# Gate and up products: two half-height terms placed in row tiles of the TensorE array

## The chip, the cores and the metric

The kernel runs on one core of one Trainium2 chip. The metric is the device time of one launch in microseconds (us). A core has TensorE (PE in the profile; its weight loads have a row of their own, PEld), VectorE (DVE), ScalarE (ACT), GpSimd (POOL) and SyncE (SP), which issues most of the transfers. TensorE multiplies a stationary operand of up to 128 rows by 128 columns (the weights, loaded by an instruction of their own) with a moving operand, whose columns stream through, and adds into PSUM.

## The reference

The whole computation is float32, S = 2048 tokens, D = 448, a hidden width of 1792:

```
a, b = xn @ dft_hid_re.T, xn @ dft_hid_im.T          # xn = layernorm(x)
h    = x + dft_seq_re @ a - dft_seq_im @ b
hn   = layernorm(h)
out  = h + (gelu(hn @ w_gate) * (hn @ w_up)) @ w_down   # gelu: tanh form
```

The change lies in the two products `hn @ w_gate` and `hn @ w_up`, which contract over 448.

## The kernel before, in words

**Numbers.** Every float32 operand is split into a float16 high part and a float16 low part (`hi_part` on ACT, `lo_part` on DVE). A product is the sum of high times high, high times low and low times high, each a float16 matmul into the same PSUM accumulator.

**Stages.** First the two Fourier products (lines L626, L498 and L691), until about 346.7 us of the span. Then gate and up (L1014), with the down product (L962) woven in from the second quarter on. Then a tail in which the last down products run alone (L1177, L1219).

**Gate and up.** The tokens are taken in four quarters (`q`) of 512, the hidden width in 14 slices of 128 for gate and for up (`f`). One pair of these is a unit `t`, 56 in all. A unit is a 2 by 2 block product: gate and up by two halves of the contraction, times those halves by two groups of 256 tokens. It is done in seven products of blocks (a Strassen form), added up in three PSUM accumulators X, Y and Z of 128 by 256. The class `GateUp` holds a unit; `product` (from L1002) writes the matmuls of one block product.

**Two kinds of product.** The contraction of 448 is cut into 256 and 192. A product over 256 has six matmuls: two slots of 128 rows times three terms. A product over 192 has one slot of 128 rows and a rest of 64 rows. Its operand on the token side is laid out in three slots: 128 rows of high part; one slot that holds the high part of the last 64 in one half of its rows and their low part in the other; 128 rows of low part. On the weight side the last 64 rows stand twice, one below the other. So one matmul with the mixed slot does high times high and high times low of the rest at once. The five terms are in `product`:

```
terms = [(0, 0, 0), (1, 0, 0), (0, 1, 1), (1, 1, 1), (0, 0, 2)]   # weight part, weight slot, token slot
```

The term (1, 1, 1) multiplies the low weights of the last 64 rows, both copies, with the mixed slot: low times high, which is needed, and low times low, which is of the size of the rounding.

**The order around the change.** The kernel is scheduled by hand: each engine executes its instructions in the order in which the Python code issues them. From the second quarter on, the PE of a unit runs: `z_open` (Z, six matmuls), eight matmuls of the down product, `xy` (Y six, X five), ten of the down product, `yz` (Y five, Z five), three of the down product, then `open` of the next unit (X six, Y six). In the first quarter there is no down product between them, and units alternate between two sets of banks; after it there is one bank each for X, Y and Z, so the next unit's first matmul on Y waits until the last reading of Y is done. `yz` runs the products A22 by T4 into Y and S4 by B22 into Z, then DVE adds Y to a kept sum (`plus(c21, ...)`, L1024), POOL multiplies it by the activated gate (L1081), and in `c12_plus` DVE reads Z (L1024 again).

**The token operands.** `ffn_hi` and `ffn_lo` fill a tile `xs` with the high and low parts, eight times in all (four quarters by two groups); `ffn_transpose` turns it by a DMA into `hops`, where rows are the contraction. T4 is the third of the three 192-row operands.

Of the kernel before, what the change touches and what calls it, by code (L numbers as in the profile page):

```python
# [32 lines left out]
def kernel(  # L33
# [40 lines left out]
    V, A, G, PE = nc.vector, nc.scalar, nc.gpsimd, nc.tensor  # L74
# [31 lines left out]
    def hi_part(dst, src, scale=1.0):  # L106
        A.activation(dst, src, AF.Copy, scale=scale)  # L107

    def lo_part(dst, src, hi, scale=1.0):
        if isinstance(scale, float) and scale == 1.0:  # L110
            V.tensor_sub(dst, src, hi)  # L111
        else:
            V.scalar_tensor_tensor(dst, src, scale, hi, op0=ALU.mult, op1=ALU.subtract)  # L113
# [43 lines left out]

    OPS_K1 = {"B11": 0, "T1": 4, "T2": 8, "T3": 12}  # L160
    OPS_K2 = {"B21": 16, "B22": 19, "T4": 22}
    N_OPS = 25
# [90 lines left out]
    def ffn_views(q, j):  # L253
        xn, t, xs = ffn[q, j]
        k1 = xs[:, 0:2048].rearrange("p (o h d) -> p o h d", o=4, h=2)
        k2 = xs[:, 2048:3200].rearrange("p (o d) -> p o d", o=3)
        return xn, t, k1, k2, t[:, 0:768].rearrange("p (o d) -> p o d", o=3)

    def ffn_hi(q, j, parts=range(2)):
        if 0 in parts:  # L260
            ffn[q, j] += (fops.tile([P, N_OPS * P], F16, tag="xs", name=f"xs_{q}_{j}"),)
        xn, t, k1, k2, t3 = ffn_views(q, j)
        if 0 in parts:
            hi_part(k1[:, 0, 0, :], xn[:, 0, 0:256])
            hi_part(k2[:, 0:2, 0:192], xn[:, :, 256:448])
        if 1 in parts:
            hi_part(k1[:, 1:4, 0, :], t3)
            hi_part(k2[:, 2, 0:192], t[:, 768:960])

    def ffn_lo(q, j, parts=range(5)):  # L270
        xn, t, k1, k2, t3 = ffn_views(q, j)
        raw, t4 = (k2[:, 0:2], xn[:, :, 256:448]), (k2[:, 2], t[:, 768:960])
        if 0 in parts:
            lo_part(k1[:, 0, 1, :], xn[:, 0, 0:256], k1[:, 0, 0, :])
        if 1 in parts:
            lo_part(k1[:, 1:4, 1, :], t3, k1[:, 1:4, 0, :])
        for n, (dst, src) in ((2, raw), (4, t4)):
            if n in parts:
                lo_part(dst[..., 192:256], src[..., 128:192], dst[..., 128:192])
            if min(n + 1, 4) in parts:  # L280
                lo_part(dst[..., 256:384], src[..., 0:128], dst[..., 0:128])

    def ffn_split(q, j):
        ffn_hi(q, j)
        ffn_lo(q, j)
# [432 lines left out]
    for k, f in enumerate(reversed(range(NF))):  # L718
        n = (17, 20, 22, 25, 27, 30, 33, 35, 38, 40, 43, 45, 48, 50)[k]
# [8 lines left out]
    for p, (n, half) in enumerate(turns):  # L728
        b, j = divmod(p, 2)
        m = (19, 24, 29, 36, 44, 52, 60)[p]  # L730
# [59 lines left out]
    first = [(jj, part, g) for jj in range(2) for part in range(2) for g in range(2)]  # L790
    for n in range(N_STEPS):
# [41 lines left out]
        if n >= FAST:  # L833

            last = n % 4 == 3
# [163 lines left out]

    TQ = 2 * P  # L1000

    def product(ps, q, t, a, b, first, last):  # L1002

        w, ops = gw[t].rearrange("p (l o d) -> p l o d", l=2, o=14), hops[q]
        wa = W_OPS[a]
        if b in OPS_K1:
            m = OPS_K1[b]

            terms = [(0, 1, 0), (0, 0, 1), (1, 1, 0), (1, 0, 1), (0, 1, 2), (0, 0, 3)]
        else:  # L1010
            m = OPS_K2[b]
            terms = [(0, 0, 0), (1, 0, 0), (0, 1, 1), (1, 1, 1), (0, 0, 2)]
        for n, (wl, ws, ms) in enumerate(terms):
            PE.matmul(  # L1014
                ps,
                w[:, wl, wa + ws, :],
                ops[:, m + ms, :],
                start=first and n == 0,
                stop=last and n == len(terms) - 1,
                skip_group_check=True,  # L1020
            )

    def plus(dst, ps, other):
        V.scalar_tensor_tensor(dst, ps, SC, other, op0=ALU.mult, op1=ALU.add)  # L1024
# [6 lines left out]
    class GateUp:  # L1031
# [9 lines left out]
            pool, tag = (ps_gu, "XYZ"[k]) if self.own else (ps_dn, f"a{k}")  # L1041
            return pool.tile([P, 512], F32, tag=tag, name=f"p{'XYZ'[k]}_{self.name}")[:, :TQ]

        def mul(self, ps, a, b, first):
            product(ps, self.q, self.t, a, b, first, True)

        def open(self):
            self.X, self.Y = self.bank(0), self.bank(1)
# [25 lines left out]
            return hh[self.q][:, n, 2 * k + g, :]  # L1074

        def yz(self):
            self.mul(self.Y, "A22", "T4", False)
            self.mul(self.Z, "S4", "B22", False)
            c21 = self.hidden(0)
            plus(c21, self.Y, self.u1)  # L1080
            G.tensor_mul(c21, c21, self.g1)  # L1081
# [64 lines left out]
    last = {}  # L1146
# [98 lines left out]
    for q in (2, 3):  # L1245
        for j in range(2):
            t0 = (q - 1) * NF + 6 * j
            for f, k, what in (
                (0, 1, lambda q=q, j=j: ffn_norm_act(q, j, hp[q, j])),
                (1, 1, lambda q=q, j=j: ffn_sums(q, j, (0,))),  # L1250
                (1, 2, lambda q=q, j=j: ffn_sums(q, j, (1,))),
                (2, 1, lambda q=q, j=j: ffn_sums(q, j, (2,))),
                (2, 1, lambda q=q, j=j: ffn_hi(q, j, (0,))),
                (2, 2, lambda q=q, j=j: ffn_sums(q, j, (3,))),
                (2, 2, lambda q=q, j=j: ffn_lo(q, j, (0,))),
                (3, 1, lambda q=q, j=j: ffn_hi(q, j, (1,))),
                (3, 2, lambda q=q, j=j: ffn_lo(q, j, (1,))),
                (4, 1, lambda q=q, j=j: ffn_lo(q, j, (2,))),
                (4, 2, lambda q=q, j=j: ffn_lo(q, j, (3,))),
                (5, 1, lambda q=q, j=j: ffn_lo(q, j, (4,))),  # L1260
                (4, 4, lambda q=q, j=j: ffn_transpose(q, j, (0,))),
                (5, 4, lambda q=q, j=j: ffn_transpose(q, j, (1,))),
                (6, 4, lambda q=q, j=j: ffn_transpose(q, j, (2,))),
                (6, 5, lambda q=q, j=j: ffn_transpose(q, j, (3,))),
            ):
                at(side, (t0 + f, k), what)

    for t in range(3 * NF, N_GU):
        f = t % NF
        if f < NF - 1:  # L1270
            n, k = divmod(f, 2)
# [36 lines left out]
    for t in range(N_GU):  # L1308
        q, f = divmod(t, NF)
# [117 lines left out]
    for k in range(7):  # L1427
        for n in range(4, NC):
            last_pair_mm(k, n, banks)
        for m, dst, sign in users.get(k, ()):  # L1430
            bank, c = banks[m]
            h, ps = drain.x[dst], bank[:, c * HD : (c + 1) * HD]
# [64 lines left out]
```

## Time and profile before

| | |
|---|---|
| median of 3 runs (lowest to highest) | 714.15 us (713.4 to 714.18) |
| the profiled execution's own time | 713.42 us |
| its span, first to last instruction | 711.6 us, so 1.8 us lie around it |
| PE busy | 706.2 us, 5517 matmuls and as many weight loads |
| granted TensorE clock, mean | 0.999 |
| gate and up, first to last matmul of L1014 | 346.7 to 678 us |

Rows of the profile have this form: line, engine, operation, output and inputs by the program's names, tile sizes, count, then busy time, the mean of one in ns, idle time before, and what ended it. A row of a timeline has the start in us and the length in us from the first start to the last end of the instructions merged in it. The end of a matmul in the records is modelled: a matmul's record is longer than the distance to the next matmul's start, because several are in the array at once. What a matmul costs in a dense stream is the distance of starts.

### The profile page before, as it was taken

Reading aid. Unit: us, or ns where it says so; the run is one execution under the profiler, and the core shown is the slowest. Engines: PE = TensorE matmul, PEld = TensorE weight load, DVE = VectorE, ACT = ScalarE, POOL = GpSimd, SP = SyncE. Lnnn points to the kernel's source line nnn. Section 1 sums busy time; section 2 is a strip of 40 time slices with the busy share of each in tenths; the row PEclk is TensorE's granted clock in tenths of the full one; section 3 lists DMA queues with packets and bytes.
Section 4 is the critical chain, followed back from the end, with each engine's and each line's share of the span. In section 5 each row is a group of like instructions: output and inputs, shape, how many; then the busy total and the mean of one; then the engine's idle time right before and its main releaser. Section 6 shows DMA issues by size and latency. Waiting matters only on the chain.

```text
span 711.6 us, 14303 instructions
## 1 busy us (share of the span) xinstructions
PE 706.2 (99%) x5517; PEld 535.6 (75%) x5517; DVE 571.5 (80%) x1194; ACT 323.5 (45%) x612; POOL 235.5 (33%) x277
## 2 busy tenths in 40 slices
PE   9999999999999999999999999999999999999998
PEld 5555555555555555897978899999999999999998
DVE  7997638696958979999667788787787877989787
ACT  5776524263617554543335444442444434354331
POOL 0000000000000000000365866576686766858441
PEclk9999999999999999999999999999999999999999
DMA  8788558999999999653698425648448576555401
GB/s 270 251 258 257 113 181 222 299 321 259 275 334 292 303 295 226 261 136 103 163 385 306 158 79 167 189 163 203 176 136 249 183 210 212 187 215 208 156 28 53
DMA packets 102613, 150.92 MB, mean 212 GB/s; under 512 B 61072, under 2 KB 72464, under 8 KB 102544
## 3 DMA queue, kind: packets, MB, share of 16 engines
q1 hardware_dynamic: 102400, 149.09, 68.0%
q10 hardware_dynamic: 144, 0.92, 0.4%
q8 instruction: 43, 0.70, 0.4%
q14 instruction: 26, 0.21, 0.1%
HBM read 115.90 MB, written 20.19 MB: 191 GB/s over the span
## 4 chain that ended last, share of the span: by engine, by line
PE 95%; DVE 2%; issue 1%; ACT 1%; DMA 0%; ACTq 0%; DVEq 0%
PE acc L626 33%; PE pY L1014 15%; PE acc_d L962 12%; PE pZ L1014 9%; PE pX L1014 9%; PE y L691 8%; PE acc_f L498 3%; PE last_a L1219 2%; PE last_X L1177 1%; PE last_tr L1177 1%; ACT ws L107 1%; DVE e L526 0%; DMA x<-in_x_dram 0%; DVE sums L452 0%; DVE sums L453 0%
## 5 line engine op out<-in xcount | busy, mean ns | idle before, releaser
L626 PE MATMUL acc<-xs,ws 128*128 128x448 f16 x1248 | 237.9, 352 | 0.3 <-DVE affine L372 0.3
L626 PEld LDWEIGHTS <-ws 128*128 128x128 f16 x1248 | 122.0, 98 | 114.3 <-ACT ws L107 0.4
L1014 PEld LDWEIGHTS <-gw 128*128 128x128 f16 x1755 | 171.5, 98 | 17.1
L209 POOL TENSOR_TENSOR wd_s<-wd 128x448 f32<-128x448 f32 x7 | 8.0, 1142 | 351.1 <-DMA wd<-in_w_down_dram 341.6
L1014 PE MATMUL pY<-hops,gw 128*128 128x256 f16 x765 | 105.3, 273 | 0.0
L962 PE MATMUL acc_d<-wd,dn_w 128*128 128x224 f16 x882 | 105.1, 259 | 0.0
L962 PEld LDWEIGHTS <-dn_w 128*128 128x128 f16 x882 | 85.0, 98 | 2.9
L113 DVE SCALAR_TENSOR_TENSOR ws<-wr,ws 128x1024 f16<-128x1024 f32 (+2 forms) x66 | 75.1, 1139 | 7.5 <-ACT ws L107 7.2
L107 ACT ACTIVATE ws<-wr 128x1024 f16<-128x1024 f32 (+2 forms) x66 | 64.4, 980 | 31.2 <-DMA wr<-in_w_seq_dram 29.6
L1024 DVE SCALAR_TENSOR_TENSOR u<-pY,u 128x256 f32<-128x256 f32 x112 | 46.9, 419 | 30.5 <-ACT c L1088 18.9
L1014 PE MATMUL pX<-hops,gw 128*128 128x256 f16 x495 | 68.7, 273 | 0.0
L1014 PE MATMUL pZ<-hops,gw 128*128 128x256 f16 x495 | 68.4, 273 | 0.0
L691 PE MATMUL y<-wh,z 128*128 128x448 f16 x336 | 66.2, 352 | 0.7 <-DVE hx L701 0.7
L1065 ACT ACTIVATE g<-pX 128x256 f32<-128x256 f32 x56 | 21.4, 382 | 81.4 <-PE pX L1014 74.2
L1052 ACT ACTIVATE u<-pX 128x256 f32<-128x256 f32 x56 | 21.4, 383 | 80.8 <-PE pX L1014 80.7
L691 PEld LDWEIGHTS <-z 128*128 128x128 f16 x336 | 32.9, 98 | 30.5 <-issue 0.9
L111 DVE TENSOR_TENSOR dn_w<-dn_s,dn_w 128x640 f16<-128x640 f32 x42 | 52.8, 1258 | 1.1 <-ACT dn_w L107 0.8
L1081 POOL TENSOR_TENSOR hh<-hh,g 128x256 f32<-128x256 f32 x42 | 31.0, 739 | 55.7 <-DVE hh L1024 53.2
L498 PEld LDWEIGHTS <-ws 128*128 128x128 f16 x504 | 48.3, 98 | 0.9
L1090 POOL TENSOR_TENSOR hh<-hh,c 128x256 f32<-128x256 f32 x42 | 38.2, 908 | 17.9 <-ACT c L1088 17.9
L1107 POOL TENSOR_TENSOR dn_s<-hh 128x256 f32<-128x256 f32 x42 | 43.7, 1040 | 0.0
L1108 POOL TENSOR_TENSOR dn_s<-hh 128x256 f32<-128x256 f32 x42 | 43.3, 1030 | 0.0
(144 smaller groups left out, 1017.5 us busy)
## 6 DMA issues: line engine op xcount, KB each, us to landing
gw<-w_dram SPq DMA_DIRECT2D x45, 896.0 KB, 5.0
wr<-in_w_seq_dram SPq DMA_DIRECT2D x100, 256.0 KB, 4.9
w_dram<-gu_w SPq DMA_DIRECT2D x14, 896.0 KB, 6.7
gu_raw<-in_w_gu_dram SPq DMA_DIRECT2D x28, 384.0 KB, 6.0
wr<-in_w_seq_dram SPq DMA_DIRECT2D x14, 512.0 KB, 5.4
wd<-in_w_down_dram SPq DMA_DIRECT2D x14, 448.0 KB, 3.9
gw_first<-w_dram SPq DMA_DIRECT2D x7, 896.0 KB, 5.6
x<-in_x_dram SPq DMA_DIRECT2D x16, 224.0 KB, 3.1
```

The lines of the kernel that those rows point to most:

```text
L107: A.activation(dst, src, AF.Copy, scale=scale)
L111: V.tensor_sub(dst, src, hi)
L113: V.scalar_tensor_tensor(dst, src, scale, hi, op0=ALU.mult, op1=ALU.subtract)
L498: PE.matmul(fast_sum(n, k), fast_a(n, i, lw, a), fast_b(j, lx, b), start=j == 0 and m == 0 and k % 2 == 0, stop=j == NT // 2 - 1 and m == ...
L626: PE.matmul(acc[key][:, :D], w[:, lw, block * P : (block + 1) * P], xs[c][:, lx, :], start=c == 0 and m == 0, stop=c == NT - 1 and m == 2,)
L691: PE.matmul(y[:, :D], z[p][:, lz, k, g * P : (g + 1) * P], wh[:, lw, k, :], start=k == 0 and m == 0, stop=k == 6 and m == 2,)
L962: PE.matmul(acc[k // 2][:, k % 2 * HD : (k % 2 + 1) * HD], a_of(la, a), b_of(lb, b), start=first and m == 0 and k % 2 == 0, stop=last and ...
L1014: PE.matmul(ps, w[:, wl, wa + ws, :], ops[:, m + ms, :], start=first and n == 0, stop=last and n == len(terms) - 1, skip_group_check=True,)
L1024: V.scalar_tensor_tensor(dst, ps, SC, other, op0=ALU.mult, op1=ALU.add)
L1090: G.tensor_mul(c22, c22, self.c12)
L1107: G.tensor_add(s[:, 0:2], t[:, 0:2], t[:, 2:4])
L1108: G.tensor_sub(s[:, 2:4], t[:, 1:4:2], t[:, 0:4:2])
```

## The change

Of the two products in `yz`, the term (1, 1, 1) is taken out of the five. The four others of Y run, then the four others of Z, and behind them two matmuls of 64 rows instead of two of 128: one for Y in rows 64 to 127 of the array, one for Z in rows 0 to 63, each with the low weights of the last 64 rows and only the high part of the tokens. The low times low part of the last 64 rows is thus left out in these two products. The two matmuls use different rows of the array and different PSUM accumulators.

So that Y's high part lies in rows 64 to 127, T4's mixed slot is turned round: low part in its first half, high part in its second. B22 and B21 keep theirs. The high parts of T4, which were one ACT instruction of 192 columns, become two of 128 and 64. The number of matmuls and weight loads is the same, and so is the order on DVE, POOL and SP.

```diff
     def ffn_hi(q, j, parts=range(2)):
...
-            hi_part(k2[:, 2, 0:192], t[:, 768:960])
+            hi_part(k2[:, 2, 0:128], t[:, 768:896])
+            hi_part(k2[:, 2, 192:256], t[:, 896:960])

     def ffn_lo(q, j, parts=range(5)):
...
-                lo_part(dst[..., 192:256], src[..., 128:192], dst[..., 128:192])
+                h, l = (128, 192) if n == 2 else (192, 128)
+                lo_part(dst[..., l : l + 64], src[..., 128:192], dst[..., h : h + 64])

-    def product(ps, q, t, a, b, first, last):
+    def product(ps, q, t, a, b, first, last, rows=None):
...
-            terms = [(0, 0, 0), (1, 0, 0), (0, 1, 1), (1, 1, 1), (0, 0, 2)]
+            terms = [(0, 0, 0), (1, 0, 0), (0, 1, 1), (0, 0, 2)]
+            if rows is None:
+                terms.append((1, 1, 1))
+            elif rows is not ...:
+                PE.matmul(
+                    ps,
+                    w[rows, 1, wa + 1, :],
+                    ops[rows, m + 1, :],
+                    start=False,
+                    stop=last,
+                    tile_position=(rows.start, 0),
+                    skip_group_check=True,
+                )
+                return
         for n, (wl, ws, ms) in enumerate(terms):
...
-                stop=last and n == len(terms) - 1,
+                stop=last and rows is None and n == len(terms) - 1,

-        def mul(self, ps, a, b, first):
-            product(ps, self.q, self.t, a, b, first, True)
+        def mul(self, ps, a, b, first, rows=None):
+            product(ps, self.q, self.t, a, b, first, True, rows)

         def yz(self):
-            self.mul(self.Y, "A22", "T4", False)
-            self.mul(self.Z, "S4", "B22", False)
+            last = (self.Y, "A22", "T4", slice(64, 128)), (self.Z, "S4", "B22", slice(0, 64))
+            for ps, a, b, rows in last:
+                self.mul(ps, a, b, False, ...)
+            for ps, a, b, rows in last:
+                self.mul(ps, a, b, False, rows)
             c21 = self.hidden(0)
             plus(c21, self.Y, self.u1)
             G.tensor_mul(c21, c21, self.g1)
```

## The prediction

> **What bounds the kernel now.** I read the page first, then the busy time by stage, then what PE waited for, then the timeline of one unit. The page says that PE is busy from end to end at the full clock, and that the chain that ended last runs through it:
>
> ```profile
> PE 706.2 (99%) x5517; PEld 535.6 (75%) x5517; DVE 571.5 (80%) x1194; ACT 323.5 (45%) x612; POOL 235.5 (33%) x277
> ...
> PEclk9999999999999999999999999999999999999999
> ...
> PE 95%; DVE 2%; issue 1%; ACT 1%; DMA 0%; ACTq 0%; DVEq 0%
> ```
>
> The windows by stage (us, then PE, PEld, DVE, ACT and POOL with counts, the granted clock, the DMA share, GB/s) show the three that hold gate and up:
>
> ```profile
> 346.70:420.00 73.30, 73.28 (x640) 62.38 (x639) 54.39 (x112) 32.81 (x68) 46.63 (x52) 1.00 0.67 227
> 420.00:590.00 170.00, 170.00 (x1629) 157.99 (x1627) 136.46 (x281) 69.73 (x167) 115.69 (x133) 1.00 0.61 185
> 590.00:678.00 88.00, 88.00 (x845) 81.78 (x843) 74.37 (x143) 37.97 (x90) 58.80 (x68) 1.00 0.55 194
> ```
>
> PE has no gap there at all. What PE waited for, over the whole span, is three waits, all outside gate and up:
>
> ```profile
> PE pw L101 <- POOL sign_t L92: 1.4, 1, 1.4
> PE y L691 <- DVE hx L701: 0.7, 1, 0.7
> PE acc L626 <- DVE affine L372: 0.3, 1, 0.3
> ```
>
> So a nanosecond more or less on PE in this stage is a nanosecond of the total, as long as nobody else becomes late. The timeline around one `yz`:
>
> ```profile
> 563.91 1.07 PEld L1014 LDWEIGHTS <-gw 128*128 128x128 f16 x10
> 564.00 0.71 PE L1014 MATMUL pY<-hops,gw 128*128 128x256 f16 x5
> 564.55 0.71 PE L1014 MATMUL pZ<-hops,gw 128*128 128x256 f16 x5
> 564.75 0.42 DVE L1024 SCALAR_TENSOR_TENSOR hh<-pY,u 128x256 f32<-128x256 f32 x1 [0.47 <-PE pY L1014]
> ...
> 565.09 0.45 PE L962 MATMUL acc_d<-wd,dn_w 128*128 128x224 f16 x3
> ...
> 565.32 0.73 POOL L1081 TENSOR_TENSOR hh<-hh,g 128x256 f32<-128x256 f32 x1 [1.19 <-DVE hh L1024]
> 565.36 0.42 DVE L1024 SCALAR_TENSOR_TENSOR c<-pZ,u 128x256 f32<-128x256 f32 x1 [0.19 <-PE pZ L1014]
> 565.38 0.82 PE L1014 MATMUL pX<-hops,gw 128*128 128x256 f16 x6
> 565.70 1.16 DVE L111 TENSOR_TENSOR xs<-tt,xs 128x768 f16<-128x768 f32 x1
> ...
> 566.03 0.49 PE L1014 MATMUL pY<-hops,gw 128*128 128x256 f16 x3
> ```
>
> Ten matmuls start between 564.00 and 565.09: 0.109 us each. The five of Y take 0.71 us, which is four such steps and 0.273 for the last one's own record. So a matmul costs a slot of 109 ns in the stream, and its record goes on for 164 ns behind its slot: two more are under way before it is done. The mean of the group says the same:
>
> ```profile
> L1014 PE MATMUL pY<-hops,gw 128*128 128x256 f16 x765 | 105.3, 273 | 0.0
> ```
>
> **The change, part by part.**
>
> *The slots.* Each of the 56 units gives up two slots of 109 ns and gets two matmuls of 64 rows. The columns streamed are still 256, so each alone lasts a slot. If they run side by side, they take one slot together: 56 x 0.109 = 6.1 us less. If one runs behind the other, nothing is saved.
>
> *The weight loads.* There are as many as before. Two of them now have to be in place for one shared slot. The nearest row for how fast loads can follow one another is the warm-up at the start, where matmuls are short:
>
> ```profile
> 4.72 0.71 PEld L101 LDWEIGHTS <-ident 128*128 128x128 f16 x12
> ...
> 4.61 1.00 PE L101 MATMUL pw<-ident 128*128 128x128 f16 x15
> ...
> L1014 PEld LDWEIGHTS <-gw x1755: 95/98/98, 383.5 to 677.7; 128*128 128x128 f16 x195
> ```
>
> Twelve loads in 0.71 us, the last of them 98 ns: (0.71 - 0.098) / 11 = 56 ns apart. Two fit in a slot of 109. How far ahead they run is shown by the one long wait of PE:
>
> ```profile
> 331.76 0.10 PEld L691 LDWEIGHTS <-z 128*128 128x128 f16 x1
> ...
> 332.76 0.73 PE L691 MATMUL y<-wh,z 128*128 128x448 f16 x3 [0.74 <-DVE hx L701]
> 332.77 0.47 PEld L691 LDWEIGHTS <-z 128*128 128x128 f16 x3 [0.90 <-issue]
> ```
>
> One load was done at once; the second came only when the waiting matmul had started, 1 us later. Loads run one ahead, at least for full height. If that holds for row tiles too, the second tile's weights start to load when the first tile's matmul starts, and its matmul comes about 56 ns after it instead of with it. Then the pair takes 109 + 56, and the saving is 53 ns a unit. For the sum I take the pair at one slot and keep 56 ns for the range.
>
> *The passage between full height and row tiles.* Every matmul and load of the kernel before has 128 rows (128*128 in each row above), so the trace has no passage from one form to the other. Now each unit has two: from the last full matmul of Z into the tiles, and from the tiles into the down product. From below the price is 0: the next matmul just takes its slot. Less is excluded, since the columns of the one before have to be in. From above it is the time from the slot's end to the end of the record, 164 ns, if the array has to run empty before its rows can be told off differently; with a load that can't be done ahead, 56 more, 220. The nearest row for a result's way out is DVE's start on Y: the fifth matmul starts at 564.44 (564.00 + 4 x 0.109), its slot ends at 564.55, DVE starts at 564.75. So 0.20 us after the slot the result is out and announced, and 164 is no mere convention. A matmul of full height still occupies all 128 rows when the first tile would start in 64 of them; that two or three are always under way makes it unlikely that the passage is free. I take the price between one missed slot, 109, and the whole way out, 164: 136 ns each way. The break-even is 109 / 2 = 55 ns each way.
>
> The Trainium skill speaks against this change here: "TensorEngine Tiling (Array Packing)", Tiling Modes, says that a change of tiling mode, as opposed to a change of tile, drains TensorE. No run here shows it yet, and it gives no time; with the whole way out as an estimate of a drain, the sum would be 725.7 instead of the 722.5 below.
>
> *The order of Y and Z.* Y's last term moves behind Z's four, so Y is ready about as late as Z. At best (side by side, free passages) the tiles' slot is that in which Z's fifth ran less one: 564.87 to 564.98, DVE can start on Y at about 565.19 instead of 564.75, ends at 565.61, then reads Z until 566.07 instead of 565.78. Who waits: the next unit's first matmul on Y, at 566.03 before and 565.92 then, so 0.3 us remain of 0.86. Queued behind on DVE is the L111 of 1.16 us, late by 0.28; the POOL product of 0.73 us comes 0.44 later, and POOL had been idle for 1.19 before it. The cover is the 0.47 and 0.19 of DVE idle time before these two. I price it at nothing. If the cover were gone, the next Y would wait for what is missing, at most 0.1 to 0.2 us a unit. With passages that cost, PE is later and the slack grows.
>
> *The T4 copies on ACT.* Eight times, one copy of 192 columns becomes two of 128 and 64:
>
> ```profile
> L107 ACT ACTIVATE xs<-xn_h 128x256 f16<-128x256 f32 x8 | 3.2, 405 | 0.0
> ...
> L107 ACT ACTIVATE xs<-tt 128x192 f16<-128x192 f32 x8 | 2.8, 350 | 0.0
> ...
> 566.24 0.38 ACT L1052 ACTIVATE u<-pX 128x256 f32<-128x256 f32 x1 [1.57 <-PE pX L1014]
> ```
>
> The first two differ by 55 ns for 64 columns, so 128 and 64 cost about 295 and 240, together 185 ns more, 1.5 us in all on an engine that in these units idles 1.57 us until PE gives it X. Nothing on the path. DMAs, and the instructions and order of DVE, POOL and SP, are unchanged; no queue is moved past.
>
> *The sum.* Per unit: 2 x 136 for the passages, less 109 for the slot: 163 ns more. Times 56: 9.1 us. Against the profiled execution's own 713.42 us: 722.5. (It stands 0.7 below the median of 714.15, so the result may lie as much higher.)
>
> **The rivals.**
>
> *Free passages, the tiles side by side.* The array takes row tiles between full matmuls as it takes any next matmul. For it: every seam between lines and shapes in the trace (256 columns to 224 and back) costs nothing. Against it: none of these changes the rows. It gives 713.4 - 6.1 = 707.3. It decides as long as a passage costs less than 55 ns.
>
> *Free passages, half a gain.* As before, but with the load one ahead: 53 ns a unit, 3.0 us, 710.4. For it: the 0.90 us of the load that was not run ahead.
>
> *The change doesn't do what it says.* The tiles run one behind the other, with free passages, or the passages eat just the slot (about 55 ns each): within 0.2% of 713.4. (0.2%, 1.4 us, is about what can be told from no change.)
>
> *Drain and exposed loads.* The array runs empty and the load comes only then: 2 x 220 - 109 = 331 ns, 18.5 us, 731.9. For it: the load at 332.77 started only when the matmul of 332.76 did; at a passage the loads may hang on the matmul before them in the same way. It is the upper end of the forecast's price and shares its chance.
>
> *DVE late.* Free passages, but Y's eviction misses the next unit's Y by more than the slack of 0.3 us in most units: needs DVE to be busy at `yz`, against the 0.47 us of idle time. With 0.2 us a unit in the 42 units that have one bank, 8.4 - 6.1: 715.7.
>
> The skill's page "TensorE: Matmul & The Clock Gate", Part 3, is on the side of the first rival: tiles in different rows start about 4 ns apart. It says so of tiles among themselves, not of the passage, and no run here shows either; by it the pair's slot is right and the first rival's time 707.5.
>
> **How the numbers follow.** A passage that costs more than it saves: 0.54, split over prices from 65 to 220 ns each way, its own range 715 to 732. Free and side by side: 0.22. Free with half a gain: 0.12. Nothing to be told: 0.09. DVE late: 0.03. The likeliest is the first, at 722.5. Faster by over 0.2%: 0.22 + 0.12 = 0.34; within: 0.09; slower: 0.54 + 0.03 = 0.57. The range goes from the first rival's 707.3 to 729, which is my price with 56 ns for an exposed load in each passage (2 x 192 - 109 = 275 ns, 15.4 us); above it I leave 0.1, below it 0.03.
>
> **What would show it.** The passage: in a timeline of one `yz`, the distance from the last full matmul of Z to the first tile, and from the second tile to the first of the down product; 109 each means free, about 245 means my price, 273 the whole way out. The pair: the distance of the two tiles' starts, near 0 or 56 or 109. The weights: whether PEld shows the tiles' two loads before the first tile starts. DVE: L1024 on Y at 0.04 us after Y's last record, and no row of PE waiting for DVE in gate and up. ACT: two rows of L107 on xs in place of the 128x192. I am wrong if the distance between the passages' ends is one slot throughout: then the rows can be told off while the array is full, and the time is 707 to 711.

## The result and the profile after

The changed kernel takes 719.73 us (median of 5 runs, 719.53 to 720.53) against 714.15 us before: 1.0087 times as long, with a 95% interval of 1.0076 to 1.0097. The execution profiled took 720.53 us, with a span of 718.7 us.

The page of the changed kernel still shows PE busy from end to end at the full clock, and what PE waited for is as short as before:

```profile
PE 713.2 (99%) x5517; PEld 526.6 (73%) x5517; DVE 581.4 (81%) x1194; ACT 324.6 (45%) x620; POOL 236.5 (33%) x277
...
PEclk9999999999999999999999999999999999999999
```

```profile
PE pw L101 <- POOL sign_t L92: 1.4, 1, 1.4
PE y L695 <- DVE hx L705: 0.7, 1, 0.7
PE pY L1032 <- DVE u L1042: 0.4, 1, 0.4
```

So neither list says where the time went: a matmul's record lasts about 273 ns, longer than any distance to the next start around the tiles (at most 213 ns), so the records leave no gap to see. The timeline of one `yz` of the changed kernel does say it (full-height matmuls are now L1032, the tiles L1021, the down product L966):

```profile
569.17 0.60 PE L1032 MATMUL pY<-hops,gw 128*128 128x256 f16 x4
...
569.61 0.60 PE L1032 MATMUL pZ<-hops,gw 128*128 128x256 f16 x4
570.13 0.10 PEld L1021 LDWEIGHTS <-gw 64*128 64x128 f16 x2 [0.21 <-issue]
570.14 0.28 PE L1021 MATMUL pY<-hops,gw 64*128 64x256 f16 x1
570.14 0.28 PE L1021 MATMUL pZ<-hops,gw 64*128 64x256 f16 x1
570.35 0.21 PEld L966 LDWEIGHTS <-dn_w 128*128 128x128 f16 x3
570.36 0.46 PE L966 MATMUL acc_d<-wd,dn_w 128*128 128x224 f16 x3
570.46 0.42 DVE L1042 SCALAR_TENSOR_TENSOR hh<-pY,u 128x256 f32<-128x256 f32 x1 [0.57 <-PE pZ L1021]
...
570.65 0.82 PE L1032 MATMUL pX<-hops,gw 128*128 128x256 f16 x6
570.91 0.42 DVE L1042 SCALAR_TENSOR_TENSOR c<-pZ,u 128x256 f32<-128x256 f32 x1
```

Read the starts. The last of Z's four starts at 569.935 (569.61 + 3 x 0.109). Both tiles start at 570.14, 3 to 4 ns apart: they do run side by side. The next full-height matmul starts at 570.36. The median over all 56 units, from the starts of the single records: 205 ns from the last full-height matmul to the first tile (204 or 205), 3 between the tiles (3 or 4), 212 from the second tile to the next full-height matmul (211 to 213). Where a slot would be 109 and the second tile's 106 to 109, 96 ns are lost on the way in and about 103 on the way out. One more detail: the full-height matmul after the way out is followed by its neighbour 10 ns late (0.46 instead of 0.45 in the row of L966 x3); its neighbour's load starts 10 to 11 ns after it, against 1 to 2 ns in a dense stream.

Together 205 + 3 + 212 + 10 = 430 ns, where before three slots of 109 took 328: 102 ns a unit, times 56 is 5.7 us. The medians are 5.6 us apart. The stage itself, from the first to the last start of gate and up, went from 331.05 to 337.17 us; of these 6.1 us, some 0.4 more are longer waits of Y on DVE in the first quarter. The rest of the 7.1 us between the two profiled spans lies before the stage: gate and up start 0.9 us later, at 347.7. In the seven runs below they start anywhere between 346.95 and 347.83, and the medians don't show this part.

The loads tell the same: before, a load of `yz` started with the matmul ahead of it. Now PEld stands idle for 0.21 us and both loads start 4 to 5 ns ahead of the first tile. Nothing is loaded ahead across the passage.

### The profile page after: what moved, and what is told of

Its sections match the earlier page's. It is cut to its first block, busy times and chain, and to the rows that moved or that the text cites. A ratio compares the mean times of both kernels' runs of the same rounds, so it can differ in the third digit from the quotient of the medians.

```text
span 718.7 us, 14314 instructions
## 1 busy us (share of the span) xinstructions
PE 713.2 (99%) x5517; PEld 526.6 (73%) x5517; DVE 581.4 (81%) x1194; ACT 324.6 (45%) x620; POOL 236.5 (33%) x277
## 4 chain that ended last, share of the span: by engine, by line
PE 95%; DVE 2%; issue 1%; DMA 1%; ACT 1%; SPq 0%; POOL 0%; POOLq 0%; ACTq 0%; DVEq 0%
PE acc L630 33%; PE pY L1032 14%; PE acc_d L966 12%; PE pX L1032 9%; PE pZ L1032 9%; PE y L695 8%; PE acc_f L502 3%; PE last_a L1241 2%; PE pY L1021 2%; PE last_X L1199 1%; PE last_tr L1199 1%; DMA hx<-in_x_dram 1%; PE pw L101 1%; ACT ws L107 1%; PE last_Y L1241 0%
## 5 line engine op out<-in xcount | busy, mean ns | idle before, releaser
L1032 PEld LDWEIGHTS <-gw 128*128 128x128 f16 x1665 | 162.3, 98 | 16.5
L966 PE MATMUL acc_d<-wd,dn_w 128*128 128x224 f16 x882 | 105.5, 260 | 0.0
L1032 PE MATMUL pY<-hops,gw 128*128 128x256 f16 x720 | 100.4, 273 | 0.0
L966 PEld LDWEIGHTS <-dn_w 128*128 128x128 f16 x882 | 81.6, 98 | 6.9
L1032 PE MATMUL pX<-hops,gw 128*128 128x256 f16 x495 | 68.7, 272 | 0.0
L1032 PE MATMUL pZ<-hops,gw 128*128 128x256 f16 x450 | 63.9, 273 | 0.0
L1130 POOL TENSOR_TENSOR dn_s<-hh 128x256 f32<-128x256 f32 x42 | 42.0, 1001 | 0.0
L1129 POOL TENSOR_TENSOR dn_s<-hh 128x256 f32<-128x256 f32 x42 | 40.3, 960 | 0.0
```

Source lines behind the costliest of these rows:

```text
L966: PE.matmul(acc[k // 2][:, k % 2 * HD : (k % 2 + 1) * HD], a_of(la, a), b_of(lb, b), start=first and m == 0 and k % 2 == 0, stop=last and ...
L1032: PE.matmul(ps, w[:, wl, wa + ws, :], ops[:, m + ms, :], start=first and n == 0, stop=last and rows is None and n == len(terms) - 1, skip_ ...
L1129: G.tensor_add(s[:, 0:2], t[:, 0:2], t[:, 2:4])
L1130: G.tensor_sub(s[:, 2:4], t[:, 1:4:2], t[:, 0:4:2])
```

## The experiments

All are edits of the changed kernel. Times are medians; each was run beside the kernel before on the same chip, which took 713.62 us in the first four and 713.44 in the last three.

**The order alone.** The last two matmuls in full height, everything else as changed.

```diff
                 PE.matmul(
                     ps,
-                    w[rows, 1, wa + 1, :],
-                    ops[rows, m + 1, :],
+                    w[:, 1, wa + 1, :],
+                    ops[:, m + 1, :],
                     start=False,
                     stop=last,
-                    tile_position=(rows.start, 0),
```

> The order of the changed kernel (four of Y, four of Z, then the last of Y and the last of Z, T4's mixed slot turned, the extra ACT copies), but the last two as full-height matmuls of 128 rows. Theory (the passages between full height and row tiles cost): no passage, so the time of before, 713.4 to 714.5 us, starts 109 ns apart throughout yz. Rival (the order costs: Y is ready later and DVE evicts it late): the changed kernel's 719.7 us or more, with rows of PE waiting for DVE.

714.44 us, 1.0012 times before (1.0003 to 1.0021). From the second quarter on, every start in `yz` is 109 or 110 ns behind the one before it. The order is not free to the last nanosecond: four waits of the first matmul of `yz` on DVE in the first quarter are longer than before and add up to the 0.8 us. (`yz` is the third use of Y in a unit, and waits until DVE has read the second. The longest is a gap of 637 ns between two starts, where DVE had been busy with a weight preparation of 1.8 us.) From the second quarter on there is none. So the order explains about 0.8 of the 5.6 us (0.2 to 1.5 by the interval), and the rest needs the row tiles.

**Both in the same rows.** No sharing, the passages as they are.

```diff
-            hi_part(k2[:, 2, 0:128], t[:, 768:896])
-            hi_part(k2[:, 2, 192:256], t[:, 896:960])
+            hi_part(k2[:, 2, 0:192], t[:, 768:960])
...
-                h, l = (128, 192) if n == 2 else (192, 128)
+                h, l = 128, 192
...
-            last = (self.Y, "A22", "T4", slice(64, 128)), (self.Z, "S4", "B22", slice(0, 64))
+            last = (self.Y, "A22", "T4", slice(0, 64)), (self.Z, "S4", "B22", slice(0, 64))
```

> Both half-height matmuls in rows 0 to 63, T4's mixed slot as before the change, so they can't run side by side; the two passages stay. Theory (passages of about 96 and 103 ns, and side by side worth one slot of 106): the second tile starts 109 ns behind the first instead of 3; 106 x 56 = 5.9 us more than the changed kernel, 725.7 us. Rival (within row tiles each load waits until the matmul before it in its rows is through, so a second tile in the same rows comes about 205 ns later): 11.3 us more, 731 us. Rival (side by side is worth nothing, the records deceive): 719.7 us.

725.6 us, 1.0166 (1.0152 to 1.018), as the first theory had it. The timeline of this run:

```profile
572.83 0.60 PE L1031 MATMUL pZ<-hops,gw 128*128 128x256 f16 x4
573.36 0.11 PEld L1020 LDWEIGHTS <-gw 64*128 64x128 f16 x2 [0.21 <-issue]
573.36 0.28 PE L1020 MATMUL pY<-hops,gw 64*128 64x256 f16 x1
573.48 0.27 PE L1020 MATMUL pZ<-hops,gw 64*128 64x256 f16 x1
573.68 0.21 PEld L965 LDWEIGHTS <-dn_w 128*128 128x128 f16 x3 [0.21 <-issue]
...
573.68 0.46 PE L965 MATMUL acc_d<-wd,dn_w 128*128 128x224 f16 x3
```

The second tile comes 0.12 us behind the first (119 or 120 ns in all units: a slot and the 10 ns that follow a passage), the way in is 205 again, the way out 202. By the starts, the way from the last full-height matmul of Z to the down product, with the 10 ns behind it, takes 205 + 119 + 202 + 10 = 536 ns a unit, against 430 in the changed kernel. So sharing a slot is worth about 106 ns a unit, as the change meant it to be; it is only less than the passages cost.

**Apart.** Each tile behind its own four matmuls: four passages a unit.

```diff
             for ps, a, b, rows in last:
                 self.mul(ps, a, b, False, ...)
-
-            for ps, a, b, rows in last:
                 self.mul(ps, a, b, False, rows)
```

> The half-height matmul of Y right behind Y's four, that of Z behind Z's four: four passages a unit instead of two, and no sharing. Theory (each passage costs): 205 ns into and 212 plus 10 out of each tile, 854 ns where before had four slots of 109; 418 ns a unit, 23.4 us over before, 737.6 us. Rival (the cost comes from the pair, two loads or two matmuls at once, and a lone tile goes like any matmul): 714 us.

736.98 us, 1.0327 (1.0313 to 1.0341): 23.4 us over before, the number expected of the price per passage. All 112 ways in are 205 ns, all ways out 211 to 213:

```profile
580.16 0.60 PE L1032 MATMUL pY<-hops,gw 128*128 128x256 f16 x4
580.69 0.28 PE L1021 MATMUL pY<-hops,gw 64*128 64x256 f16 x1
580.90 0.61 PE L1032 MATMUL pZ<-hops,gw 128*128 128x256 f16 x4
...
581.44 0.28 PE L1021 MATMUL pZ<-hops,gw 64*128 64x256 f16 x1
581.66 0.46 PE L966 MATMUL acc_d<-wd,dn_w 128*128 128x224 f16 x3
```

A lone tile pays the same as a pair. The price hangs on the change between full height and tiles, not on the pair.

**Three pairs.** The pair issued three times between the same two passages.

```diff
-            for ps, a, b, rows in last:
-                self.mul(ps, a, b, False, rows)
+            for n in range(3):
+                for ps, a, b, rows in last:
+                    product(ps, self.q, self.t, a, b, False, n == 2, rows)
```

> The pair of half-height matmuls is issued three times instead of once (the low-times-high term of the last 64 rows is then added three times, so the sums differ by that); the passages stay two a unit. Theory (the cost is in the passages, and within row tiles a pair goes in one slot): two slots of 109 ns more a unit, 12.2 us, 731.9 us. Rival (loads run only one ahead, so a pair has to wait for its second load): about 165 ns a pair, 18.5 us more, 738.2 us. Rival (every pair costs what the first one did, about 215 ns): 24 us more, 743.8 us.

732.5 us, 1.0264 (1.025 to 1.0278), 0.6 us over the first theory. Its timeline:

```profile
518.51 0.22 PEld L1021 LDWEIGHTS <-gw 64*128 64x128 f16 x6 [0.21 <-issue]
518.52 0.28 PE L1021 MATMUL pY<-hops,gw 64*128 64x256 f16 x1
518.52 0.28 PE L1021 MATMUL pZ<-hops,gw 64*128 64x256 f16 x1
518.64 0.27 PE L1021 MATMUL pY<-hops,gw 64*128 64x256 f16 x1
518.64 0.27 PE L1021 MATMUL pZ<-hops,gw 64*128 64x256 f16 x1
518.75 0.27 PE L1021 MATMUL pY<-hops,gw 64*128 64x256 f16 x1
518.75 0.27 PE L1021 MATMUL pZ<-hops,gw 64*128 64x256 f16 x1
518.95 0.21 PEld L966 LDWEIGHTS <-dn_w 128*128 128x128 f16 x3 [0.21 <-issue]
518.95 0.46 PE L966 MATMUL acc_d<-wd,dn_w 128*128 128x224 f16 x3
```

Within the tiles the next pair comes after 0.12 us once and 0.11 from then on. All six loads lie in 0.22 us: in tiles, both loads of the next pair run ahead, one for each half of the rows. So a pair costs a slot, and only the passages cost more: by the starts the two added pairs take 219 ns a unit, 12.3 us.

**The same in full height.** Each last term three times, all in 128 rows: the edits of the first and of the fourth run together.

```diff
-                    w[rows, 1, wa + 1, :],
-                    ops[rows, m + 1, :],
+                    w[:, 1, wa + 1, :],
+                    ops[:, m + 1, :],
...
-                    tile_position=(rows.start, 0),
...
+            for n in range(3):
+                for ps, a, b, rows in last:
+                    product(ps, self.q, self.t, a, b, False, n == 2, rows)
```

> The same terms as in the run with three pairs (each last term issued three times), but all in full height, so there is no passage: six slots of 109 ns where there were three pairs in tiles. Theory (two passages cost about 209 ns together, a shared slot saves 106 to 109): four slots more than the full-height order run of 714.4 us, 109 x 4 x 56 = 24.4 us, 738.9 us, so with three pairs the tiles are faster, 732.5 against 738.9, and the point at which both are equal lies at two pairs. Rival (something other than the passages cost in the changed kernel, and tiles stay behind): 732 us or less.

738.79 us, 1.0352 (1.0335 to 1.037): where three pairs are to be run, the tiles are 6.3 us faster (732.5). At one pair they are 5.3 us slower than the same order in full height (719.73 against 714.44; 4.8 if each is taken against its own time before). A line through the two differences crosses zero at about 1.9 pairs; two pairs were not run.

**Shorter tiles.** Only the first 128 of the 256 columns stream through the tiles.

```diff
-                    ps,
+                    ps[:, 0:P],
...
-                    ops[rows, m + 1, :],
+                    ops[rows, m + 1, 0:P],
```

> The changed kernel, but each half-height matmul streams only the first 128 of its 256 token columns (the low-times-high term of the last 64 rows is left out for the other 128). Theory (a passage is a fixed time behind the last column that streams in): the way out of the tiles starts 54 ns earlier, about 158 ns after the tile's start instead of 212; 3.0 us less than the changed kernel, 716.7 us. Rival (a tile matmul holds the array for a fixed time, whatever it streams): 212 ns as before, 719.7 us.

717.41 us, 1.0052 (1.0037 to 1.0067); the total is 0.7 us over what the first theory gave (about 0.2 of it are longer waits of Y on DVE in the first quarter), but the gap is the one that it gave: 158 or 159 ns out of the tiles in the units with a down product, 158 to 160 in the others, and 205 in.

```profile
567.93 0.23 PE L1021 MATMUL pY<-hops,gw 64*128 64x128 f16 x1
567.93 0.23 PE L1021 MATMUL pZ<-hops,gw 64*128 64x128 f16 x1
568.09 0.46 PE L966 MATMUL acc_d<-wd,dn_w 128*128 128x224 f16 x3
```

So the way out is a fixed time behind the last column, not a fixed time of a tile.

**The down product ahead of the tiles.**

```diff
-        def yz(self):
+        def yz(self, between=lambda: None):
...
+            between()
             for ps, a, b, rows in last:
                 self.mul(ps, a, b, False, rows)
...
-        cur.yz()
-        cur.c12_plus()
-        dn_mm(d, range(18, 21))
+        cur.yz(lambda: dn_mm(d, range(18, 21)))
+        cur.c12_plus()
```

> The changed kernel, but from the second quarter on the three matmuls of the down product that followed yz run ahead of the two tiles, so the last full-height matmul before the tiles has 224 columns instead of 256, and the first behind them 256 instead of 224. Theory (a fixed time of about 96 ns behind the last column): 192 ns into the tiles instead of 205, the way out at 212 as before, nothing else: 719 to 720 us. Rival (the passage can be hidden, or its price depends on what the neighbours are or on whether they belong to the same accumulator): clearly other gaps. A side cost is possible: Y is ready three slots later, and the next unit's first matmul on Y may wait for DVE.

720.35 us, 1.0094 (1.0078 to 1.0109), not to be told from the changed kernel.

```profile
569.86 0.45 PE L966 MATMUL acc_d<-wd,dn_w 128*128 128x224 f16 x3
570.24 0.28 PE L1021 MATMUL pY<-hops,gw 64*128 64x256 f16 x1
```

Behind 224 columns (a slot of 96) the way in is 191 or 192 ns in all 42 units that have a down product; behind 256 columns, in the 14 others, it stays 204 or 205. Again 96 ns behind the slot, whether the neighbour belongs to Z or to the down product. The way out stays at 212. The 13 ns saved in 42 units are 0.5 us, and the total doesn't show them, for a side cost came too, though not where it was expected: from the second quarter on, eight `yz` wait 57 to 79 ns for DVE's reading of Y before their first matmul, 0.7 us in all. In the changed kernel none does there. So with these neighbours the price stays.

Not tried: a unit that stays in row tiles throughout, with every full-height matmul cut into two halves. Both halves would add into one accumulator from two row tiles, and no run here shows whether they may.

## Why the prediction was right

The result, 719.73 us, lies on the side forecast and in the range; the point, 722.5, was 2.8 us too high. The increase itself was put at 9.1 us and is 5.6: the sum started from an execution 0.7 us below the median, and that hides 0.7 us of the 3.5. The side had a chance of 0.57, and the range held faster times too; what bears the forecast out is the passage, not the range.

- *PE bounds the stage, a nanosecond there is a nanosecond of the total.* Right: 102 ns a unit times 56 gives 5.7, the medians give 5.6.
- *The pair takes one slot.* Right, 3 ns apart; the run with both in the same rows shows the 106 ns that this is worth. The rival with half a gain, loads one ahead, was wrong about tiles: loads ran ahead for both halves of the rows. The row it went by, a full-height load that waited 0.90 us, said nothing about tiles.
- *The passage costs more than it saves.* Right, and this decided the sign. Its size was the term mis-sized: the prediction took 136 ns each way, between a missed slot and the whole 164 ns by which a record outlasts its slot. Measured are 96 in and 103 out, and 10 for the slot behind. With 96 + 103 + 10 - 109 + 3 = 103 ns the sum would have been 713.4 + 5.8 = 719.2. The error was to look for the price between those two rows: the first tile starts 205 ns behind the last full-height matmul, whose record lasts 273. One missed slot, the lower of the two, was no bound either.
- The Trainium skill, "TensorEngine Tiling (Array Packing)", Tiling Modes, says that changing the mode drains TensorE. The runs agree that each change costs, 96 to 103 ns; whether that time is a drain, no run shows. The Trainium skill, "TensorE: Matmul & The Clock Gate", Part 3, puts tiles in different rows about 4 ns apart; 3 to 4 were measured.
- *Loads at a passage.* They aren't done ahead, as the rival with exposed loads feared, but it costs no 56 ns: the matmul starts 4 to 5 ns behind its load, and what is left is the 10 ns at the next. A load's record lasts 92 to 98 ns, about the price of a passage, so one may ask whether the price is just that load. The kernel before has two late loads in full height, with no tiles about. The one at 5.88 us had waited for ACT while no matmul was running, and its matmul starts 4 ns behind it:

```profile
5.88 0.49 PEld L626 LDWEIGHTS <-ws 128*128 128x128 f16 x4 [0.45 <-ACT ws L107]
5.89 4.33 PE L626 MATMUL acc<-xs,ws 128*128 128x448 f16 x22 [0.28 <-DVE affine L372]
```

The other starts at 6.61, 46 ns before its matmul, which still comes 189 ns behind the one ahead, a usual slot for 448 columns. So by the starts of the records the 96 ns lie ahead of the loads and are not the time of a load; what the loads wait for, they don't show.

- *The order of Y and Z costs nothing.* Right from the second quarter on: DVE starts on Y 0.1 us after the next full-height matmul and PE doesn't wait. Wrong by up to 0.8 us in the first quarter, which the prediction hadn't looked at, as the run with the order alone shows; in the changed kernel about 0.4 of it is left, with PE later there.
- *The ACT copies cost nothing.* Right; they take 298 and 243 ns (295 and 240 were estimated):

```profile
L107 ACT ACTIVATE xs<-tt 128x128 f16<-128x128 f32 x8 | 2.4, 298 | 0.0
L107 ACT ACTIVATE xs<-tt 128x64 f16<-128x64 f32 x8 | 1.9, 243 | 0.0
```

## What to carry to other kernels

A matmul of 64 rows among matmuls of 128 is a change of the array's form, and each change costs about 100 ns of PE here, behind the last column, beside all the neighbours that were tried; a matmul of half the rows alone is dearer, by 209 ns, than one of full height with half of it wasted. A pair of row tiles into two accumulators is worth one slot, so at 256 columns it takes about two pairs between two changes to come out even (worked out, not run), and three gain. Such a loss is seen neither in PE's busy share nor in its waits: count the distance of starts where the form changes. PEld's row points to the place: 0.21 us idle before each pair of tiles.

## What was not expected of the hardware

In row tiles the weight loads run ahead for both halves of the rows, so that two loads and two matmuls go in each slot of 109 ns; in full height one load ran ahead. And the two changes of form cost nearly the same: 96 ns on the way in; on the way out 103 after a single pair, 93 after three pairs, the 10 between them being the late second slot behind the way in. Both are less than the 164 ns for which the records go on. Why it is these 93 to 96 ns, and which part of the array they are spent in, no run here tells.
